# Two layers of sliding-window attention and a token-mixing MLP on one core: another order of operations and another choice of engines

## The chip, the core and the metric

The kernel runs on one core of one Trainium2 chip. The metric is the device time of one execution in microseconds (us). Four engines compute: TensorE (PE; its weight loads are shown apart as PEld), VectorE (DVE), ScalarE (ACT) and GpSimd (POOL). SyncE (SP) only issues DMAs, one after the other.

## The reference

The input x has 2048 tokens of 512 numbers. The block below is applied twice, with the same weights; all data are bfloat16.

```
def _A_ref(x, wqkv, wo):
    H = 32; Dh = D // H; W = 256
    q, k, v = (x @ wqkv) split in three, 32 heads of 16
    scores = q k^T * 0.25, masked to 0 <= i - j < 256
    return softmax(scores) v, heads joined, @ wo
def _B_ref(x, w1, b1, w2, b2):
    h = _layernorm(x)
    u = gelu(einsum("bsd,sf->bdf", h, w1) + b1)      # mixes tokens: 2048 -> 1792
    return (einsum("bdf,fs->bds", u, w2) + b2) transposed
x = x + _A_ref(_layernorm(x), ...)
x = x + _B_ref(_layernorm(x), ...)     # and both lines once more
```

## The kernel before

The program first builds a graph of 2477 operations and then writes them down in an order that a table gives. An operation is one compute instruction, or a few: a group of two or four matmuls, a DMA or a set of DMAs. The table `ORDER` is a packed list of 2477 pairs. `begin_order` (L42 on) unpacks it. The first number of a pair says which operation comes next, the second which of its ways is taken where it has several (`alts`). `Graph.replay` goes through the list, appends each operation to the queue of its engine, and hands out buffers: a tile gets, at its first operation, the buffer that has been free longest, and it gives it back after its last one. So the table fixes five queues, the engine of every operation with a choice, and which earlier operation a buffer is waited for. `Graph.emit` then places the semaphore waits. Each engine works through its queue in order: an operation that waits holds up everything behind it in that queue.

The work per layer is this.

- **Layer norm.** For each tile of 128 tokens, DVE takes statistics (L478, L480), POOL the power -0.5 (L491), DVE normalises (L498).
- **Queries, keys, values.** Four groups of 512 tokens. The normalised tile is turned by a DMA (L549; the first four tiles by PE), PE projects (L520), DVE or ACT takes the results out of PSUM (L585, L587, L610, L612, L651, L653). Keys go to `kbd`, where the two heads of a 32-row strip stand side by side with zeros between: through `stg` by eight DMAs (`f_kz`, L620), or by two masked instructions on DVE or POOL (L626). Values go through `vst` to `vb` by four DMAs (`f_vz`, L656).
- **Attention.** 76 score steps in each layer. PE writes scores into four PSUM banks (L710), ACT takes the exponential of them in two instructions (L725), POOL multiplies by a 0/1 mask or DVE takes a bitwise and (L746), PE multiplies with the values (L767). The quotient follows (L787 to L798), with the product on POOL or DVE (L793). The score steps keep their order among themselves.
- **Fillers.** Between two score steps PE runs projections of the next group, the output projection (L809 takes it out) and, for the first 4 and then the next 8 of 16 row blocks, partial sums of the first MLP product (`u_part`, L873, L877). In the second layer these partial sums cover 8 row blocks; the second MLP product of the first layer, too, runs as filler there (L929).
- **MLP.** `u_last` (L888) does the remaining row blocks, DVE adds the partial sum (L899), ACT does the gelu (L903), `y_block` the second product, DVE adds it to x (L929), a DMA writes the result.

The weights of the first MLP product are loaded by `load_w1` (L823) into four buffers of `w1b`, 128 KB a DMA. In the first layer's second `u_part` there are seven column groups of four loads; they are called g0 to g6 here, and g0.1 is the first load of g0. The second product's weights are loaded by L835 into `pt` and `w2b`. All loads stand in SP's one queue, along with the copies of keys and values and the turning of tiles.

Of the kernel before, what the change touches and what calls it, by code (L numbers as in the profile page):

```python
# [11 lines left out]
P = 128  # L12


ORDER = (
    'c-qxgO^EB(6+W`>WbTwZpa*)OfF3AC3kB4ofC38W6}70KfLioG1r=OSK?@fga6knIToA=A4!A)9FC0+81s5D}zyU8@@WKl(Cg8;sW-$vFrr^RXX7LuY7|JYq'
    'Jho>%Z(jah+C`6Mbg%CJ`ObH~>qaOwd7$sPNdoX|UDto1$8SXu@w@>1XTIxF#~p+GMz8;l2`0-jN@Vv<rB++^er(HNn&qRT`B4;AgE*K@r_A?l|Cz0M#@l_<'
    'R0L5Jwa!Q+R1k!Vv<d{W7A_KvTb0OvRx8!hYOUK4SlQOwhRz>GaS;4KW$Z9?sVrNDq3Et83A(JyB7Lk~P<nkPDsp1Z6h#sRfazpHDe!!+&F4IM{`|R!I|<3v'
    'mGAo}IS&9|94%+#_;j(D3KA9mKA9LM93LN3oYs@(5Qej<6ig-^Ny_uQmmTAjWurA8D+;9Zd5Z4Izs0t4c`z7CAjWaOC(Ae$y3iq{*&uc;<?1Ou<+9L1OMFwH'
    'l#%L;pAt4EaYRUoSi!%;AhfI?2*RKB`+W-!SeQ(D?~Y<SHcKtXX_%!b3{B&y7nGusX-3hzs>ug@7`h=?wx$7vV}>us8BZo-7}=6-_if<~H`jTQ=XrQSs3c4E'  # L20
    'I*^1Xq9jJql`Myh2|O8|oSqO$RrULdX_<>f`;>yBzR_v{@B+?lG$2m_E&;NvhS9ymhV*o~I6aO^C3*~n_VT>dnw>3|U(9B+PN`iznaxg4-MV{ndNel-!yaMy'
    'N0T@{9#7)g%$A1YUxm*<oA##@!-$RHM}x>HHJgUf&ay0RWi8J$-1f>o{Lo-5&}wBCt7;sVW6QGe2!gPz3qk-VC)H}D8mtUq2}>9Y82SSYxeGw8r?z9GUzC=F'
    '(^EzIImqbEcszc@gC<F=oB!~2k+nMln<5#qdcD%D5!(ivizCy%!8stLV(2=tEJD1uU7g5^q7b6#ntpM8O^6CGIPI(Iyf+&4fQQ%d0LW{uQA@IV3l8?uYL!(O'
    'jUkM}5~03NJlFFa-^QbP?|1~qD~e@tAPC0L=y!XBlKI?tj(p2UW@mxMn0|htGr{!~0BLq4eabK}?Lj;HOSjw2GWb)gm9ZvskzcOs!uuB=yq{1yx65VA^E}J-'
    'sQa#)Q(4z#nM$~ZRFa-ZZA6P93dkC5$^;l4U(5;aegX|a!es1@oiO(pq0Of2K#b;-S;cWkDI8iNnDusQw2~wYY*CU;O%oK_0H!d@m4xZkkwjI;Hbs<#tk>&h'
    'Ld!uSHJgowopvQ!19g=T8RcEoA(+oVYy?j9MG$VR+3eDMgb)lm9q6|6yseMNgUaCZ80g9vPi>!C7Ntp|Fm`Z&l3-hi;*%0pHB}%bUH1cD_dH5@9LP*_#yXby'
    'w1pI6tcJ)`-b#6N>oAIbT5=qRRjY??89faI2W-~@o-tWg<R=IlL!!vCETs|y70wl9xzsdeWk*LxGYx=~&gYga4F-eu0At#{ILpx+7}V>7!A#3CLYS|r;U9kA'
    '#sv;wf$M@&E(1&^wZE<Wm#-^V6_s6FT!^aj7_P1iW6ps__{G_9xI9x;b#dmp1Gf*9{Ah}_gHPdbI2v*YoQ>Olf-HspC*#R@wQoyWD&}xR$aUcgl3Ie+ZZ@0q'
    '1UuPyk|Z_MBqp*j`z2%SnU_GbS#6Av^R=3o)WmYxab4y*wh%aSHwXg&)PGyo8HXrSpoX<diRE&!P)-SfCzuhVCzx}LM^5U-d9&4=KWZ%VT+<Ex@p9ShJo;k>'
    'GNoS}(bp+oMq#0&6$M<>qMR3nk1@4vL7<?4s+yzcKRE_s5PFGuFg<eJJ!kkP01|01h<F3jmC`1j8CtDWQPievWtrG)@_Z`wP@SNgUo|c-FO^QNC}(HcsGT8I'  # L30
    '6BIEps@0_0m8(@<$5e$l3_~n^&-dg~sU#ZMrfK6bDkiMXBX`?8W#~M`oRfKp=U3!JEDTB4B~8;-4UYv8Rb{yZeRz60;(5~RF-6Xmj!ZJC|B)mUR9qsI6TDF%'
    '5JkLKW}JX>e29TF44&YfbA5e%$WN8Mi;K?)A>A(e(Cz*i^%Odt4hM}^tAbWfE4^M7$(p9A8JHxot3)?-FbvZ$Kz*t@rj2{+E9Yb)2xWM@%BLubc+b1?&<7ud'
    'oHG0DU;nf(ul}*<ot(h&f+&<o5=v98HW6`hp2NpN3-vee=D8{eAIiT&_6P!e(5?c5@^A10s#f2RDtPzBWye8b_J8F&j_2Iu+{zq;3@_iw1jmCcbrB{05#Q?f'
    '(Yc(<a5u6?9EazyyBjLX!c%q94uFcXZl+gedv-oU%w-HTfd&#D>Z2qX)>c<hT1h%d+sdj*t&%1US&qxqa;(TK3`b)!9t;SuZm;VH7+REzDDK&IVEa}SnW^a}'
    'cv<kikN1*hxGENgi85hm8fF4BbWNmfK~(zyDe0h8^ht&0X{y(QIMyS%LQ96mAEBB@Vsu4mNJ#%&UCQ8{k4B@;ktFf0>tj*Sdo`XyehzfJ7?0ca1i9k$w62zG'
    'ie`*QooW?zQFGl!qn@@F<2W7;hjFtRcN0W4Q7x<F`!_!cf=ZyOb^J--*{-Uq2nnhsphmCKO<rjsd?(}Xf1$0*oxat_y1MtmWU^Z)yUXk@PdMZ>_EV0mm)!>_'
    '?&D71TW^Ss`!_W#_gB@e?Qa&|+w4V(H?8Y2#o~74y7|5p)<v=KGM`_==gX~7xVHql!0p1s-9ziP<aY79`F=2ke03CF<G61XIF7ql;W%ywcJ859g^g2%!cH66'
    '?R@b>xJu#X`7*j}UHys!ZXx=nZWX>+Klchu=e})LtclO<hIe-%j^p6}*bZNPDtkb!&Hws!%d`hMwYQycGZbK3KE$89i^AsnCJdWMti)y|DcmZlc2jTNaWC77'
    '#oJ1;c++}NJixD;KYSe=6mQ2B*WoSRb;G*4UF4=*9~qBce37*~dGu1hHqaC{+O~#jzp!`b^Fs!{kb2xcswsKxR&lqwyGCS3<hXk<tPalYc(egz0}Jd*=#J~R'
    'WB1@*<BKj8H&OkXWL^_wt3rj%Y;H$LA8f*Xoe17tQiT;e3NIVMaW75QS4m%PSJ1WscXw@aJ9>OOU~_}q@pP*z#d{a-_K>?G^WT*i?p0<yJOcNs`*Ppm<hyt6'  # L40
    'Rt&f;;4fHV`zoxf+jrr1@@6h~N1~VBo&OVo{}2Aq9P0'
)  # L42

def begin_order(n):
# [965 lines left out]
```

## Time and profile before

| what | value |
|---|---|
| three runs | 436.65, 437.78, 437.89 us (median 437.78) |
| the profiled execution, its own time | 437.46 us |
| its span, first to last instruction | 435.7 us |
| granted TensorE clock | 1.000 |
| PE busy | 422.4 us, 6185 matmuls |
| ACT busy | 315.7 us |
| DVE busy | 319.3 us |
| POOL busy | 188.3 us |
| 128x512 matmul, shown duration | 381 ns |
| exponential of 128x1024, shown duration | 1047 ns |
| bytes moved by DMA | 46.17 MB |

The shown duration of a matmul overlaps the next one. Six 128x512 matmuls in a row take 1.40 us in the chain, and 26 of them 5.72 us, so they start 0.216 us apart. The same holds for exponentials: 40 in a row take 36.97 us in the chain, 0.92 us each. A stretch is read by the engine that has no idle time in it.

### The profile page before, as it was taken

Reading aid. Unit: us, or ns where it says so; the run is one execution under the profiler, and the core shown is the slowest. Engines: PE = TensorE matmul, PEld = TensorE weight load, DVE = VectorE, ACT = ScalarE, POOL = GpSimd, SP = SyncE. Lnnn points to the kernel's source line nnn. Section 1 sums busy time; section 2 is a strip of 40 time slices with the busy share of each in tenths; the row PEclk is TensorE's granted clock in tenths of the full one; section 3 lists DMA queues with packets and bytes.
Section 4 is the critical chain, followed back from the end, with each engine's and each line's share of the span. In section 5 each row is a group of like instructions: output and inputs, shape, how many; then the busy total and the mean of one; then the engine's idle time right before and its main releaser. Section 6 shows DMA issues by size and latency. Waiting matters only on the chain.

```text
span 435.7 us, 14338 instructions
## 1 busy us (share of the span) xinstructions
PE 422.4 (97%) x6185; PEld 188.9 (43%) x6185; DVE 319.3 (73%) x620; ACT 315.7 (72%) x360; POOL 188.3 (43%) x280
## 2 busy tenths in 40 slices
PE   8989889999989999999999999999999999999997
PEld 6544333443334444444344444444444444445443
DVE  7999888798786888656778998779879757522133
ACT  6999999999996952604989999999999970520000
POOL 5967757656662510010374566777455241000000
PEclk9999999999999999999999999999999999999999
DMA  8763223212054248742462550331224144776433
GB/s 253 196 126 72 58 66 85 62 25 56 15 139 114 72 124 228 204 101 48 89 146 67 129 128 5 63 75 23 47 61 116 53 136 124 194 201 181 138 89 129
DMA packets 103002, 46.17 MB, mean 106 GB/s; under 512 B 33308, under 2 KB 102940, under 8 KB 102940
## 3 DMA queue, kind: packets, MB, share of 16 engines
q1 hardware_dynamic: 102940, 45.26, 40.7%
q8 instruction: 49, 0.80, 0.8%
q14 instruction: 13, 0.11, 0.1%
HBM read 33.56 MB, written 2.10 MB: 82 GB/s over the span
## 4 chain that ended last, share of the span: by engine, by line
PE 77%; ACT 19%; DMA 2%; DVE 1%; issue 0%; SPq 0%; POOL 0%
PE PS L520 54%; ACT pt L725 18%; PE PS L888 8%; PE PS L710 8%; PE PS L767 7%; DMA w1b<-in_B_w_dram 1%; DMA x_sb<-in_A_x_dram 0%; SPq L823 0%; DVE stats L478 0%; ACT kbd L595 0%; DVE stg L610 0%; POOL rstd L491 0%; DVE oT L798 0%; ACT xhT L569 0%; ACT qT L587 0%
## 5 line engine op out<-in xcount | busy, mean ns | idle before, releaser
L725 ACT ACTIVATE pt<-PS 128x1024 bf16<-128x1024 f32 (+1 forms) x304 | 280.6, 1035 | 12.8 <-PE PS L710 11.9
L746 POOL TENSOR_TENSOR pt<-pt,ldm 128x256 int32<-128x256 int32 (+2 forms) x199 | 132.2, 684 | 92.8 <-ACT pt L725 92.1
L520 PE MATMUL PS<-xh_sb,w1b 128*128 128x512 bf16 x280 | 70.0, 381 | 1.6 <-DMA w1b<-in_B_w_dram 1.5
L520 PE MATMUL PS<-xhT,wqkv 128*128 128x512 bf16 (+1 forms) x288 | 67.8, 357 | 2.0 <-ACT pt L725 1.3
L520 PE MATMUL PS<-uT,w2b 128*128 128x512 bf16 (+2 forms) x308 | 67.5, 360 | 0.0
L710 PE MATMUL PS<-qT,kbd 32*128 32x64 bf16 (+4 forms) x1552 | 60.2, 247 | 3.0 <-ACT pt L725 1.2
L929 DVE SCALAR_TENSOR_TENSOR x_sb<-PS,bcol,x_sb 128x512 bf16<-128x512 f32 x31 | 22.7, 744 | 44.7 <-PE PS L520 44.6
L491 POOL TENSOR_TENSOR rstd<-agg,mhalf 128x2 f32<-128x2 f32 (+1 forms) x33 | 24.2, 736 | 67.0 <-DVE agg L480 66.8
L710 PEld LDWEIGHTS PS<-qT,kbd 32*128 32x128 bf16 x1552 | 22.6, 92 | 62.1 <-ACT pt L725 42.0
L787 DVE STREAM_TRANSPOSE rl<-PS 128x1024 f32<-128x1024 f32 x32 | 39.8, 1244 | 11.7 <-PE PS L767 11.6
L767 PE MATMUL PS<-pt,vb 64*17 64x128 bf16 (+4 forms) x3104 | 44.2, 248 | 1.7 <-issue 0.7
L478 DVE BATCH_NORM_STATS2 stats<-x_sb 128x6 f32<-128x512 bf16 x64 | 43.2, 682 | 0.8 <-DMA x_sb<-in_A_x_dram 0.2
L903 ACT ACTIVATE uT<-rl,bcol 128x512 bf16<-128x512 f32 x28 | 18.1, 711 | 34.7 <-DVE rl L899 34.7
L520 PEld LDWEIGHTS PS<-uT,w2b 128*128 128x128 bf16 x308 | 27.5, 98 | 31.2 <-issue 2.9
L520 PE MATMUL PS<-uT,pt 128*128 128x512 bf16 x168 | 39.7, 379 | 0.0
L767 PEld LDWEIGHTS PS<-pt,vb 64*17 64x17 bf16 x3104 | 31.8, 84 | 17.5 <-issue 8.5
L520 PEld LDWEIGHTS PS<-xh_sb,w1b 128*128 128x128 bf16 x280 | 23.6, 97 | 32.8 <-issue 6.6
L888 PE MATMUL PS<-xh_sb,w1b 128*128 128x512 bf16 x168 | 37.4, 379 | 0.0
L520 PEld LDWEIGHTS PS<-xhT,wqkv 128*128 128x128 bf16 x288 | 23.9, 97 | 29.4 <-issue 6.2
L520 PE MATMUL PS<-wqkv,xhT 128*128 128x512 bf16 x128 | 34.2, 381 | 0.0
L520 PE MATMUL PS<-wo_sb,oT 128*128 128x512 bf16 x128 | 33.1, 381 | 0.8 <-ACT pt L725 0.5
L746 DVE TENSOR_TENSOR pt<-pt,ldn 128x256 int32<-128x256 int32 (+2 forms) x67 | 27.3, 420 | 5.2 <-ACT pt L725 5.1
(64 smaller groups left out, 332.6 us busy)
## 6 DMA issues: line engine op xcount, KB each, us to landing
w1b<-in_B_w_dram SPq DMA_DIRECT2D x112, 128.0 KB, 3.0
w2b<-in_B_w_dram SPq DMA_DIRECT2D x70, 128.0 KB, 3.0
pt<-in_B_w_dram SPq DMA_DIRECT2D x42, 128.0 KB, 3.0
vb<-vst SPq DMA_DIRECT2D x64, 68.0 KB, 2.1
out_dram<-x_sb SPq DMA_DIRECT2D x15, 128.0 KB, 1.8
x_sb<-in_A_x_dram SPq DMA_DIRECT2D x3, 512.0 KB, 5.9
kbd<-stg SPq DMA_DIRECT2D x88, 16.0 KB, 1.9
wqkv<-in_A_wqkv_dram SPq DMA_DIRECT2D x4, 256.0 KB, 4.1
```

Of the source, the lines that this page charges most:

```text
L478: op("vector:stat", lambda e: e.bn_stats(st[:, 0:6], x_sb[:, t, :]), reads=[f"x{t}"], writes=[("st", i)], cost=dve_cost(512))
L491: op("gpsimd:rstd", lambda e: e.tensor_tensor(rstd[:, t0:t1, 0], agg[:, t0:t1, 1], mhalf[:, 0:1].to_broadcast([P, t1 - t0]), op=ALU.pow), ...
L520: return e.matmul(o, lhsT=w, rhs=x, start=start, stop=stop, skip_group_check=True)
L710: last = e.matmul(bank(tt[r // 2], r % 2)[:, base + c0 * 64:base + (c0 + n) * 64], lhsT=kbd[32 * r:32 * r + 32, tk.slot, o, jj].rearrange( ...
L725: op("scalar:exp", lambda e, ts=ts, tp=tp, i=i, cols=cols: e.activation(probs(tp)[:, i, 0:cols, :], pair(ts)[:, :, 0:cols].rearrange("p r ...
L746: return e.tensor_tensor(v, v, m, op=by)
L767: last = e.matmul(bank(t, h)[32 * r:32 * r + 17, i + q0 * 64:i + (q0 + n) * 64], lhsT=vb[64 * h:64 * h + 64, tk.slot, jj, 4 * o + r, :], r ...
L787: op("vector:od", lambda e, t=tod, tr=tr: e.transpose(rl[:, tr.slot:tr.slot + 2].rearrange("p a b -> p (a b)"), pair(t)), reads=[(tod, i) ...
L888: last = e.matmul(bank(tu, tt), lhsT=v()[:, sc - b0, k0 + tt * P:k0 + (tt + 1) * P], rhs=xh_sb[:, sc, :], start=(sc == b0), stop=(sc == NT ...
L903: op("scalar:gelu", lambda e, ft=ft, tt=tt: e.activation(uT[:, ft, :], rl[:, tmps[tt].slot], ACTF.Gelu_apprx_tanh, bias=b1col[:, ft:ft + 1 ...
L929: op("vector:resy", lambda e: e.scalar_tensor_tensor(x_sb[:, t, :], bank(ft), b2col[:, t:t + 1], x_sb[:, t, :], op0=ALU.add, op1=ALU.add), ...
```

## The change

Only the table `ORDER` is different; every other line stays, line numbers too. The graph is the same 2477 operations with the same dependences.

```
 ORDER = (
-    'c-qxgO^EB(6+W`>WbTwZpa*)OfF3AC3kB4ofC38W6}70KfLioG1r=OSK?@fga6knIToA=A4!A)9FC0+81s5D}zyU8@@WKl(Cg8;sW-$vFrr^RXX7LuY7|JYq'
...
+    'c-pmAPl)5@6@Rk7>3*Aj1Dc|M7PLhH6?9NQ0TmQbKmi35(1HUF_@ICbK8WIi4_;6~0Uca$zzYs2;DQ%iP{9Qi9B{w|7v|uDTlV0C3qH(Y0zSAffuYP{4twac'
...
 )
```

Unpacked, the two tables compare as follows (number of operations on each engine, where it has a choice):

| operation | before | after |
|---|---|---|
| attention mask (L746) | POOL 199, DVE 67 | POOL 178, DVE 88 |
| keys into `kbd` (L620, L626) | SP 11, DVE 9, POOL 4 | SP 8, DVE 7, POOL 9 |
| quotient's product (L793) | POOL 21, DVE 11 | POOL 22, DVE 10 |
| queries, keys, values and partial sums out of PSUM (L585 to L590, L610 to L614, L651 to L653, L873, L875) | DVE 107, ACT 16 | DVE 109, ACT 14 |
| keys straight to `kbd` (L595, L600) | DVE 7, ACT 2 | DVE 6, ACT 3 |
| zeroing a half of `kbd` at the start (L468, L469) | ACT 2, POOL 1 | ACT 1, POOL 2 |
| the ones column of `vst`, a part of the mask (L442, L463) | DVE 1, POOL 1 | POOL 1, DVE 1 |

In all, 120 operations change their engine. ACT has 358 operations before and 356 after, DVE 611 and 630, POOL 269 and 255, SP 311 and 308.

PE's queue holds the same 928 operations. The 152 score steps keep their order. From score step 12 to 60, and from 84 on, the operations between two score steps are the same but for single fillers that move by a step. Before step 12 products with the values and projections stand elsewhere by one or two steps. In the two MLPs the groups of two matmuls are interleaved in another way: products of the second kind begin earlier beside the last ones of the first kind.

SP's queue is the one that changes most. Around the second `u_part` of the first layer:

```
before: g1.1 (18.8 us) ... g1.4 (61.8) ... g1.2 (88.2) ... g2.1 (102.7), keys x2,
        values, g6.2, g0.3, g2.3, g2.4, g0.2, g1.3, g0.1, values, g0.4, g2.2, ...
after:  g1.2 ... g1.1 ... g1.3 ... keys x2, g1.4, ..., g2.2, ..., keys, g2.4, one w2 load,
        g0.1, values, g0.2, g5.1, g0.3, g2.1, g0.4, g2.3, ...
```

The exponentials of a score step's two halves change places in many steps. One eviction of values that stood on ACT at 118.05 us (L653) stands on DVE behind L791 and ahead of L610. On DVE at the start, one L478 and one L480 stand ahead of the L585 that was at 9.60 us, and the L585 of 11.84 us goes to ACT in place of the one that was there at 11.81 us. In the last MLP the matmuls of the fifth loaded column group of `u_last` stand ahead of those of the seventh in PE's queue; they stood behind them before.

More of the change, by code (lines that the diff above doesn't have):

```diff
@@ L15 @@
 ORDER = (
[L16 to L39, printed above, removed]
@@ L40 @@
-    'WB1@*<BKj8H&OkXWL^_wt3rj%Y;H$LA8f*Xoe17tQiT;e3NIVMaW75QS4m%PSJ1WscXw@aJ9>OOU~_}q@pP*z#d{a-_K>?G^WT*i?p0<yJOcNs`*Ppm<hyt6'
-    'Rt&f;;4fHV`zoxf+jrr1@@6h~N1~VBo&OVo{}2Aq9P0'
+    'c-pmAPl)5@6@Rk7>3*Aj1Dc|M7PLhH6?9NQ0TmQbKmi35(1HUF_@ICbK8WIi4_;6~0Uca$zzYs2;DQ%iP{9Qi9B{w|7v|uDTlV0C3qH(Y0zSAffuYP{4twac'
+    'Ju|j<v-#6(pDpXt_rCAbd++yq@3~Rpn>=_Bh6Hq!;>W}*m%;Oj#iII=>$-HL*v_xuU9;Eic0n_Kt$UB+n5|YT+D)9qsX5iSP*!|WIvs!Lk47WwJxg=lOp#^F'
+    'vOp4XTUU}K!me>32;H7At5)0oC+(!&>1G{K^20c`T<JkjsZi>dsm7EdacPAR+j?kOqIM)pk{}UDmSv(4o*a`I&u(NgKFtUvWH9IrSk}L~zLE$CYw^#ot_p=h'
@@ new lines @@
+    ';H)lYCZ)&cXXJD|8;{4+>6D=SJsY2neP1pOhO(TH^BPIJr1Mnx?DNH9p(tbqGYKFF&g0<AAPfE)^s|1@PZc7|oem+C(zYbETDs~$+ipa$`1>dfL#`<_DJ7rK'
+    'u!gT;r`1AGt=6gxU#Nd<+jeRAXf)!A1*`u78aJ8PuGcM>%f2(UdQIE*Bi{!T3Z}6^!1WBnu?^RA?e`1|-8BpYK-JWdWepfmNYfs4b(QCtA_LR`L{SXG6R52)'
+    '<V+GvrAtxd#@^^YJ(}Ay%2fK6ESo5c_8ewPt0hS?x+w?{$6bgZyH3-qtLx|Ob{JlTjm8<ApPik>|LR^ql3bAK>iqotAJeIyB=h-V(eS+K91ok%=hf=PeBlJn'
+    ';;Z?f-_OZuCT7#=Unp8^_<okO`~6nS?{un$5gYANDQdU8Cx1W^B+W*XF+Gae?=(#aT({vg8nS%ZYzjV;fAgQ2Uz^QJrFsxR5elUOAUTJHVyWMU4>2NQ45nq8'
@@ new lines @@
+    'x<M)Xt*EHp^clSnM8c0x_$<?985k2-yVXV!0BZO~MjQv6z;<gjM8p=E;2habMYliTi<BBJXtJW1rgBZGZCs8gb7E47l5w1#sVR?0DynkSNaJR+*Gh=oI64YN'
+    'p<W9}z?X^dAC)LYYzt1IU|Uw@8M2cc;TFppT12`prTsoh)ATtI;Q6tsf6eRKwYCs1FUV|7OyGwZOeTz_y&(*Tqi(U^|MS{wxhr%#aqIwCjhbNDb{I|p9wS9Y'
+    'j$H7(M~}dDL9~q~2zc}<FY!F`!7UYBQ9_Vmfu^ihYwp6R+X+LQ0)n~UY(~v`os>$k5)_MpUn*J*G=M0!EQJzkXcbK_mkV0S15I@`W>Z7e^hB>wN$RSKpS9cR'
+    'fQVg5k;)pa*W*}-qFSw3w7~RC-gS$Gx@(#Q(^zBI*9-~mdXv&A^2R+AylFOLLkx+mMq}}BqKrmMV*ROP+s$S<ibS5pCeI53Vj`SW0>lakk)-F!L(CBXx^(G@'
@@ new lines @@
+    'ZNsx?E_vp@YuiaeZO69bnBMma-rGSCyfd#jPQ`JH2ym@N-5{W}OkC}qw>3>ObX_GpFY}7RBU@OLQJ|tAP>K~t0hrA&nI1@3Ivz+vl*xFAi6($3{ZSN!w4QdV'
+    's!AG-K>~%i*HbRO!9%e=hydeoB!5*G#R3#+t}L-*38cm42^=q%7Yvrm`;s)u1|v){NlG!6<GF3Gk?QHc7!9-jXjCrqFb3**Ubp*8j=*OFsVOI|R_jTx*F&;M'
+    '*VjGLgHM;sFpOZaNSa9JAUvH+#@XcbaTG>zLty1H<^az`G4@!gUiUovedajt^M#UcIVh4@*hCUk)lyZ!jMlFKOcz!wSPHVB0=&sEA_z=&<@K-9)DY7&5#Z}-'
+    'FV?kVZFQmnU35A!A(&*07x-kHB;boukxK=#dM-RII8IrVuqVtt?;}e2iJ=`0D4oq`h&&RZRHFBhpUCcqSjjWSo`TnRJI+%lP0S*+-)tud;vwU)^5;@YX+K4K'
@@ new lines @@
+    '(>~f;M_Fj`tc8sPpc2+=wOYN~>()V+wT)jsfZ_m_NRzqi8mc=kRS_b+fnhWZeVwBkasU_tE>Izw8@6G{hCz=t4ZUUrkruJLEtg9{H}rmgfH|!H^Q6l<h&{nq'
+    'L<p@ImCGkQ6vc8`5>G@r90~%*(iD2?T)n33^73?iU*d*%OqSsu^!!gxCzBAkC+qrzW`7ECqu;Nl2#Oc4>$HWL;`%=J*OZt<a~+-6?DvRiMwrKj`L;eFX!ir`'
+    'A%c%#=iGG(aKv+mEx%d9Ih<Xck;Q8DZ-Si_yRi7>aC|yBH4IT7>taXCGK4g1eenf6`65X^NAT8do`&_u^`?UXdR&33rfarc0k`lmCbVU#hUVC&<2tH(t=i6}'
+    'h>*7)Je2r{4|tyE7&~Uz3YAWRSyF}P!DVRMjDcZI0sAU;EdmTLstFfNSxTWG42F@=?3KIo^<hwNgpDMwHlx_DRNAdpy;k+2a)6prtzN8##ZnQ<BJX;9(`|aO'
@@ new lines @@
+    '8v#bk25R~~Q^C+ccb$S)t-8{=qA2rnsi2s^OD<-mwN5UIg`Flt8R;yny3uO&yw;?vt7NtES&gnDI}(cxzQN8*OIHwz=Ryhl^7XmRW}&9@(_&8@PU>tdr2{FO'
+    '&(pLvDi)iC27xTgW|^U+aCVA+emdCfu+_?j+=`;8L5piRk#1qNBimK*B~vP3H`6o|s#Pfnq>Aq8m^||4&&@hYYg_T!JpEMRIN&ySxc%i|H{`gRHMc@uIsi$2'
+    'Fo_R@+YZpWp8*yp+)r+2@W`zi?r|Ggk5IP5djR?TT6y%wcFp$8{Jq`yyCg^Oh3oH&lFz+*4@y2yArHB44-asA&qv!mHzC<Yhuh4qU0nxs6V%&n9K0UMAH851'
+    'cZb<_d<RnwzSWn_eD1*Wz1zOAH^$$d^U`4)960_8Qtj-6-1h<Z^5fBWaP~(M{73KQxV<dk?oPOi_|9{V`zi2pua6zCM~)9}JL+w|`)h7FliTFaj$OG!?%fh>'
@@ L42 @@
+    'v*ajukapXP+f4p^S9ZAlwA#V94)hxw-12JOS~u6GvTRY<jJAaa<pp52Wd(0HzU1>Scz8d*IeepjL3y_`e;0<0L%YN|48n_~zSZ4n?j0&~d%oV=5q9mw&%T9U'
+    'WLtF)A93R4mHCZ2pT8OG*RfkC^SCX)hwjV1-v*52UQXDx8M)1lgDP^E%iGV6GTWuOJrcY!A6}JShqJl6KE)lr`KB7bM5dpRue-v>-3|8Y!cAq^y=YH!Qx&&%'
+    '-deWRk;A2THTeHm9e!9SevlE|{~pQj)9oX=7t+1Ba|eKI%*}0o@Rr+hAeZBA@!Boq_QAVVeqYai4S4()i034d'
 )
```

## The prediction

> **What bounds the kernel now.** The first view is busy time by windows that follow the stages.
>
> ```profile
> 9.00:117.00 108.00, 101.38 (x2036) 44.36 (x2036) 94.26 (x189) 107.49 (x122) 76.00 (x111) 1.00 0.37 82
> 117.00:160.00 43.00, 41.27 (x875) 18.90 (x873) 34.29 (x63) 35.88 (x39) 19.04 (x26) 1.00 0.37 98
> 160.00:215.00 55.00, 55.00 (x315) 23.80 (x300) 37.06 (x67) 22.15 (x30) 6.03 (x9) 1.00 0.56 146
> 215.00:356.00 141.00, 140.67 (x2520) 59.34 (x2519) 116.06 (x229) 135.13 (x149) 81.79 (x117) 1.00 0.32 79
> 356.00:436.00 80.00, 76.85 (x384) 36.19 (x382) 31.11 (x52) 9.84 (x16) 1.39 (x2) 1.00 0.52 148
> ```
>
> The columns after the window are its length, then busy time of PE, PEld, DVE, ACT and POOL, then PE's granted clock. From 9 to 117 us ACT is idle for 0.51 us of 108, PE for 6.62: the exponentials set the pace. From 117 on it is PE: 1.73 idle to 160, none to 215, 0.33 to 356; the 3.15 in the last window are mostly its ends. The clock is 1.00 everywhere. The change leaves PE's 928 operations and all exponentials in place, so an order can only win idle time: 0.5 us of ACT before 117, 1.7 + 0.3 us of PE to 356, and little behind.
>
> The second view, the chain of waits, agrees, and names one load:
>
> ```profile
> 42.99 36.97 ACT pt L725 x40
> ...
> 125.75 4.67 DMA w1b<-in_B_w_dram
> 130.46 1.90 PE PS L520 x8
> ...
> 160.17 5.72 PE PS L520 x26
> ```
>
> The third, the timelines of PE, ACT and SP around that place, gives its price and its cause:
>
> ```profile
> 130.46 1.90 PE L520 MATMUL PS<-xh_sb,w1b 128*128 128x512 bf16 x8 [1.52 <-DMA w1b<-in_B_w_dram]
> ...
> 132.74 1.94 ACT L725 ACTIVATE pt<-PS 128x1024 bf16<-128x1024 f32 x2 [2.26 <-PE PS L710]
> ...
> 116.00 1.24 SPq L620 DMA_DIRECT2D kbd<-stg  x2
> 118.67 3.81 SPq L656 DMA_DIRECT2D vb<-vst  x4
> 122.52 3.71 SPq L823 DMA_DIRECT2D w1b<-in_B_w_dram  x7
> ```
>
> PE stands 1.52 us, and ACT 2.26 behind it. The load is g0.1, issued at 125.75 as the last of the seven: SP first spent its time on a copy of keys and 3.81 us on a copy of values. It then took 4.67 us to land, one of the slowest of its line:
>
> ```profile
> DMA to landing us min/median/max: 2.1/3.0/4.9
> ```
>
> **The change, part by part.** The sum starts from the profiled execution's own 437.46 us, 0.32 under the median of 437.78; the runs lie 1.2 apart. About 0.3% (1.3 us) is what a measurement of this kernel can tell from no change, so faster means under 436.47 and slower over 439.09.
>
> *g0.1 goes ahead of the values copy.* In the new SP queue it stands behind the copy of keys (done at about 117), one w1 load and one w2 load, about 0.5 us each. It is issued at about 118, and even with 4.9 us it lands by 123; its matmuls would begin 0.216 us (the spacing of matmuls) after the ones at 128.34 and 128.55, so at 128.8. The hole goes: 1.52, and the 0.381 shown for the last matmul before it shrinks to its 0.216, another 0.17. PE has 0.33 us of idle time from 160 to 356, so what is won here is carried to the end. **-1.7.** The three loads fill the 1.43 us for which SP stood before the values copy (117.24 to 118.67). The copy itself waits for an eviction that now ends on DVE at 118.99 instead of 118.64, so it begins 0.33 later: the last of its DMAs, issued at 120.66 before, then lands by 120.66 + 0.33 + 3.2 (the longest here) = 124.2, and its reader, a PV product, starts at 124.79. Behind it the loads g0.2, g5.1 and g0.3 are needed later than g0.1 was, each at least 3.5 us from issue to use. If one of them is late, the hole moves instead of going; that is the first rival.
>
> *The start.* One L478 (0.69) and one L480 (0.18) are put ahead of the L585 of 9.60, with 0.65 to 0.8 us delay. That is the queries of the second score step, whose matmuls start at 10.11; they can then start at 10.9 or 11.0, and the exponentials that wait for them stand ready from 11.95, as the four at 9.03 end then. With 0.8 us from scores to exponential that leaves 0 to 0.3 of ACT idle, and as much again where the exchange of L585 and L587 near 11.8 (0.38 and 0.40) reaches the exponentials. ACT sets the pace here, so it passes one to one. Bounds 0 and +0.5; **+0.3**, nearer the upper one since queues don't step aside.
>
> *An eviction of values moves from ACT (118.05, 0.59 long) to DVE.* DVE is idle for 0.70 from 118.29 to 118.99 between L791 and L610, so it fits. ACT's time is worth something only if ACT sets the pace, and from 117 PE does: **0**, bound -0.65.
>
> *120 operations change engine.* DVE gets 6.2 us more, POOL loses 5.7, ACT 1.1, from their rows' means. In 9 to 117 DVE goes from 94.3 to about 99.6 of 108. What covers it: DVE still has 8 us over, and between the end of a mask and the PV product that reads it lie 3.5 us at the median; under 0.6 in 11 of 99. PE waits for POOL's masks before L767 four times, 2.2 us in all, at places where PE waits for ACT anyway. **0**; without the cover see the third rival.
>
> *Keys.* Three copies fewer go through SP, at 5.5 to 6 us of its time each, and POOL does five more. This eases SP where weight loads queue. The copy through SP that is left with the least room lands in about 7.3 us against 7.8 to its reader: **0**.
>
> *A fetch of instructions.* PE stops for 0.54 us in the middle of one product at 116.31, with no operation to wait for. The same 2,107 matmuls stand ahead of it afterwards, so it may stay: **0**, bound -0.54.
>
> *The last MLP.* The fifth column group of `u_last` now goes ahead of the seventh, so its buffers' loads have less time. Before, from the issue of a load to its reader there were 3.7 us or more. Laid out with 0.216 us a matmul, six loads now have 2.8 to 3.5, mean 3.2: two of the fifth group (sixteen matmuls, 3.3 to 3.5, less 0.5 for the second, which SP issues later) and four further on. What landings took there, first `w1b` from 369 to 378, then `w2b` and `pt` from 377 to 406:
>
> ```profile
> DMA to landing us min/median/max: 2.1/2.8/3.8
> ...
> DMA to landing us min/median/max: 2.2/2.9/3.4
> ```
>
> At the medians only the tightest is missed, by 0.1. Bounds 0 and 6 x (3.8 - 3.2) = +3.6; **+0.2**, by the medians.
>
> These loads move 128 KB. The Trainium skill, "DMA: Bandwidth & Descriptors", section "Anatomy of one DMA — SWDGE (gpsimd) path", gives about 2.0 us plus the bytes over 436,000 a microsecond, for another issuing path; an estimate by it is 2.3 us, by which no load is late and this term is 0. The trace's medians are 0.5 us above it, so the trace does not agree.
>
> Sum: 437.46 - 1.7 + 0.3 + 0.2 = 436.26, so **436.3**.
>
> **The rivals.**
>
> *No difference.* The load's hole closes and something else takes its place: one of the loads behind, or ACT, which has only 7.1 us idle in 117 to 160, 2.26 and 1.09 of them at this hole. Or the hole is not in every run: 4.67 us of landing is far above the median, and with 3.0 the load would have been there at 128.8, in time. Then only the start's cost is left: 437.46 to 437.8, and with half of the gain 436.9. For it: the hole's load is a slow draw. Against: the draw's median just meets the need, and the spread of the three runs is of the hole's size. Taken over, 436.5 to 439.
>
> *Slower, by the last MLP.* PE is the only engine at work there, so each late load is paid in full. With the burst's 3.8 for all six it is 437.46 - 1.7 + 0.3 + 3.6 = 439.7. It decides (over 439.09) from a mean landing of 3.2 + 3.03 / 6 = 3.7 us. Against it: 2.8 and 2.9 as medians. For it: the DMA engines are busiest here, and the tight loads stand in bursts.
>
> *Slower, by DVE and POOL in each other's way.*
>
> ```profile
> L746 POOL TENSOR_TENSOR pt<-pt,ldm 128x256 int32<-128x256 int32 x141 | 102.9, 743 | 61.1 <-ACT pt L725 60.6
> ...
> L746 DVE TENSOR_TENSOR pt<-pt,ldn 128x256 int32<-128x256 int32 x49 | 20.8, 431 | 5.2 <-ACT pt L725 5.1
> ```
>
> Of POOL's masks of 128x256, those alone have a median of 0.727 us; nine that overlap a DVE mask have 0.904. In 9 to 117 there are 18 more masks on DVE. If each costs its neighbour 0.18 and PE's product and then ACT waits for it, that is 3.2: 436.3 + 3.2 = 439.5. It decides from 0.155 each (2.8 / 18). If a mask held POOL for DVE's whole 0.431, it would be 7.8, and 444. Against it: POOL has 32 us idle there, and its waits are for ACT.
>
> The Trainium skill, "SBUF — State Buffer", section "SBUF: two separate sides", says that a DVE instruction with two SBUF inputs and a GpSimd one that reads SBUF lock each other out for the whole instruction; that rule speaks against this change. The nine rows agree in sign, and at 0.18 they show less than a full lock.
>
> **How the numbers follow.** The forecast, 434 to 436.47, gets 0.43: one measured hole with a cause that the new queue removes, at a gain near the bound. No difference gets 0.26. The late loads get 0.20, DVE and POOL 0.11. The lower end is 433.8: 437.46 less 1.7, 0.65, 0.54 and most of ACT's 0.5 before 117, less 0.3 for the draw of a run. The upper end is 440.5, the two slower cases with 0.8 for a spread between runs. Likeliest alone: 435 to 437. Faster 0.43, same 0.26, slower 0.31.
>
> **What would show it.** Right: no wait of PE L520 for `w1b` near 130, g0.1 issued near 118, ACT without the 2.26, and the chain from 160 on shifted earlier by 1.3 to 1.7 with PE at 55.0 of 55 behind. The start: ACT idle 0.2 to 0.4 between 9 and 22. The last MLP: PE's waits for DMA in the last 80 us in sum, 0.2 by the forecast and 3.6 by its rival. The masks: POOL's mean over 743 and ACT below 107 of 108 by the third. Wrong: the first score step of layer two no earlier than before, or PE idle by over 1 us anywhere behind 160.

## The result, and the profile after

The changed kernel is slower: 438.48 us, median of 20 executions, against 437.20 of 20 executions of the kernel before; ratio 1.003, 95% interval 1.0016 to 1.0045. The forecast was 436.3. The profiled execution of after took 437.81 us (span 436.1), so it is one of the quicker ones. The 20 executions of before lie 2.7 us apart, those of after 4.6, and so one profile of each can't show a difference of 1.3. In the runs below, a few executions far outside the rest (480 to 2283 us; one of 528.44 had a granted clock of 0.755) are left out of the ratios.

The first reading is the windows of after, columns as in the prediction.

```profile
9.00:117.00 108.00, 97.89 (x2029) 44.88 (x2049) 98.22 (x199) 107.13 (x123) 74.06 (x109) 1.00 0.35 80
117.00:160.00 43.00, 41.67 (x873) 19.40 (x880) 33.21 (x63) 36.11 (x39) 20.75 (x29) 1.00 0.41 110
160.00:215.00 55.00, 53.43 (x296) 23.19 (x300) 35.69 (x67) 24.32 (x33) 7.55 (x12) 1.00 0.50 136
```

DVE went from 94.3 to 98.2 (about 99.6 was forecast), and ACT from 107.5 to 107.1 of 108, as forecast. The third row is new: before, PE was busy for 55.00 of 55. (This trace has 6117 of 6185 matmuls, so busy PE is a little low elsewhere too; waits are safer to read.)

The second reading is the timeline around the old hole, PE, then ACT, then SP.

```profile
128.36 2.44 PE L520 MATMUL PS<-xh_sb,w1b 128*128 128x512 bf16 x10
...
131.18 1.94 ACT L725 ACTIVATE pt<-PS 128x1024 bf16<-128x1024 f32 x2 [0.67 <-PE PS L710]
...
118.92 1.70 SPq L823 DMA_DIRECT2D w1b<-in_B_w_dram  x1
120.67 2.62 SPq L656 DMA_DIRECT2D vb<-vst  x4
```

PE runs through, and ACT idles 0.67 instead of 2.26: g0.1 is issued at 118.92, ahead of the values. At 148.4 us PE is 1.50 ahead of the profile of before. The third reading, PE's timeline further on, shows where this went.

```profile
187.08 1.04 PE L520 MATMUL PS<-uT,pt 128*128 128x512 bf16 x4 [1.09 <-DMA pt<-in_B_w_dram]
...
377.35 1.90 PE L888 MATMUL PS<-xh_sb,w1b 128*128 128x512 bf16 x7 [0.52 <-DMA w1b<-in_B_w_dram]
```

The first is in the first layer's MLP, of which the prediction said nothing, the second in the last MLP. Before, PE ran through at both places; at the second its timeline has one unbroken row:

```profile
373.91 10.52 PE L888 MATMUL PS<-xh_sb,w1b 128*128 128x512 bf16 x48
```

In SP's and DVE's timelines the cause of the first can be read:

```profile
171.82 0.47 SPq L835 DMA_DIRECT2D pt<-in_B_w_dram  x1
179.49 1.40 SPq L835 DMA_DIRECT2D w2b<-in_B_w_dram  x3
180.93 0.47 SPq L823 DMA_DIRECT2D w1b<-in_B_w_dram  x1
181.44 0.47 SPq L835 DMA_DIRECT2D w2b<-in_B_w_dram  x1
181.96 1.50 SPq L835 DMA_DIRECT2D pt<-in_B_w_dram  x3
...
178.79 0.68 DVE L899 TENSOR_TENSOR rl<-PS,w2b 128x512 f32<-128x512 f32 x1
```

SP issues nothing from 172.3 to 179.49. The `w2b` load at the head of its queue needs a buffer that holds a partial sum, and DVE's L899 reads that one at 178.79, until 179.47. The load of `pt` that PE wants sits six places behind the head: issued at 182.48, landed 4.56 us later. Nobody needs the load at the head before 185.40. The old queue stands there for 2.4 us only:

```profile
169.58 2.48 SPq L835 DMA_DIRECT2D pt<-in_B_w_dram  x5
174.50 0.37 SPq L835 DMA_DIRECT2D w2b<-in_B_w_dram  x1
```

### The profile page after: what moved, and what is told of

Same layout as the page of the kernel before. It is cut to its first block, busy times and chain, and to the rows that moved or that the text cites. A ratio compares the mean times of both kernels' runs of the same rounds, so it can differ in the third digit from the quotient of the medians.

```text
span 436.1 us, 14244 instructions
## 1 busy us (share of the span) xinstructions
PE 412.8 (95%) x6117; PEld 188.4 (43%) x6185; DVE 324.3 (74%) x637; ACT 315.4 (72%) x359; POOL 183.2 (42%) x271
## 4 chain that ended last, share of the span: by engine, by line
PE 70%; ACT 19%; DMA 4%; DVE 3%; issue 2%; SPq 2%
PE PS L520 48%; ACT pt L725 19%; PE PS L710 8%; PE PS L888 7%; PE PS L767 7%; DMA x_sb<-in_A_x_dram 1%; DMA pt<-in_B_w_dram 1%; DMA w1b<-in_B_w_dram 1%; DVE stats L478 1%; DVE rl L899 1%; SPq L835 1%; DMA vb<-vst 0%; SPq L656 0%; DVE xh_sb L498 0%; ACT L959 0%
## 5 line engine op out<-in xcount | busy, mean ns | idle before, releaser
L746 POOL TENSOR_TENSOR pt<-pt,ldm 128x256 int32<-128x256 int32 (+2 forms) x178 | 119.5, 689 | 96.3 <-ACT pt L725 96.0
L520 PE MATMUL PS<-xhT,wqkv 128*128 128x512 bf16 (+1 forms) x276 | 66.1, 356 | 4.4 <-ACT pt L725 2.3
L520 PE MATMUL PS<-xh_sb,w1b 128*128 128x512 bf16 x266 | 66.9, 380 | 2.2 <-issue 1.7
L491 POOL TENSOR_TENSOR rstd<-agg,mhalf 128x2 f32<-128x2 f32 (+1 forms) x33 | 23.0, 698 | 61.1 <-DVE agg L480 61.0
L478 DVE BATCH_NORM_STATS2 stats<-x_sb 128x6 f32<-128x512 bf16 x64 | 43.0, 685 | 1.2 <-DMA x_sb<-in_A_x_dram 0.4
L520 PE MATMUL PS<-uT,pt 128*128 128x512 bf16 x165 | 41.0, 379 | 1.5 <-DMA pt<-in_B_w_dram 1.1
L746 DVE TENSOR_TENSOR pt<-pt,ldn 128x256 int32<-128x256 int32 (+2 forms) x88 | 35.3, 421 | 6.5 <-ACT pt L725 6.4
L888 PE MATMUL PS<-xh_sb,w1b 128*128 128x512 bf16 x164 | 37.4, 379 | 0.8 <-DMA w1b<-in_B_w_dram 0.5
L520 PE MATMUL PS<-wqkv,xhT 128*128 128x512 bf16 x116 | 32.2, 380 | 2.1 <-issue 1.1
L793 POOL TENSOR_TENSOR ul<-rl,rc 128x512 bf16<-128x512 f32 x22 | 23.8, 1081 | 22.7 <-DVE rc L791 21.8
```

The source lines that it names most:

```text
L478: op("vector:stat", lambda e: e.bn_stats(st[:, 0:6], x_sb[:, t, :]), reads=[f"x{t}"], writes=[("st", i)], cost=dve_cost(512))
L491: op("gpsimd:rstd", lambda e: e.tensor_tensor(rstd[:, t0:t1, 0], agg[:, t0:t1, 1], mhalf[:, 0:1].to_broadcast([P, t1 - t0]), op=ALU.pow), ...
L520: return e.matmul(o, lhsT=w, rhs=x, start=start, stop=stop, skip_group_check=True)
L746: return e.tensor_tensor(v, v, m, op=by)
L793: f_n = lambda e, tr=tr, tl=tl: e.tensor_tensor(ul[:, tl.slot].rearrange("p (q x d) -> p x q d", x=2, d=16), T(tr)[:, :, :, 0:16], R(tl).u ...
L888: last = e.matmul(bank(tu, tt), lhsT=v()[:, sc - b0, k0 + tt * P:k0 + (tt + 1) * P], rhs=xh_sb[:, sc, :], start=(sc == b0), stop=(sc == NT ...
```

## The experiments

All compare with the kernel before on the same chip. The theory after the first profile: what was won by 150 us was lost in the two MLPs, at one load each. The rivals were that loads set the pace there whatever their order, that the loss is spread over the many engine choices, and that chance made the profiles. A cut between the orders is made where both have the same work on PE behind them.

**One stretch at a time.** First, the new first part alone:

```diff
-up to 151.6 us: order of before
+up to 151.6 us: order of after
 from there on: order of before
```

> The new order up to the product that starts at 151.6 us before (150.4 after), the old order from there on, the whole first MLP and layer 2 included. Theory A (the gain is made in the first 150 us and lost by the new queues of the two MLPs): up to the cut the two profiles differ by -1.5 us, and with the old first MLP this is kept to the end: 437.2 - 1.5 = 435.7. Theory B (the first MLP's loads set the pace whatever their order, so PE that comes earlier only waits longer for them): nothing is left, 437.2. Theory C (the loss lies in the many engine choices of the first 150 us and the profile of after was a lucky draw): 438 or more.

Measured: 437.03 against 436.98 us, ratio 1.0001 (0.9985 to 1.0016). Its profiled execution was 1.1 us ahead of the profile of before at 148 us and stayed so to the end. So in this execution nothing is lost in the old MLPs (theory B has no support there), yet the median shows no gain, and the 435.7 of theory A lies outside the interval (436.3 and up): the 1.5 was measured from one execution of before.

```diff
 up to 151.6 us: order of before
-151.6 to 216.7 us: order of before
+151.6 to 216.7 us: order of after
 from there on: order of before
```

> The old order up to 151.6 us, the new one for the first MLP and the start of layer 2 (to 216.7 us), then the old one again. Theory A: SP stands 7.2 us for one load of the second product's weights, whose buffer holds a partial sum until L899 reads it; the loads behind it come late and PE waits 1.1 us plus the 0.2 that overlapping matmuls hide: 437.2 + 1.3 = 438.5. Theory B (PE came too early): PE comes 1.5 us later here, so the loads are in time, 437.2. The profile also shows whether the hole of 1.5 us at 130 us and the stop of 0.54 at 116 us, both in the untouched part, are there in another execution.

Measured: 439.99, ratio 1.0051 (1.0031 to 1.0070). The loss is there, but the cut adds to it: at 156.33 us PE waits 0.95 for an L877 that stands behind two L498 on DVE, which no whole kernel shows. Of the wait at 187 us it has 0.43. And in the untouched part the hole at 130 us is 1.03 us, not 1.52, and the stop at 116 us isn't there. In layer 2, again in the old order, PE waits 0.85 at 290.59 for a copy of values that took 3.8 us to land; the profile of before has no wait there, the tenth run 0.25.

```diff
 up to 355.8 us: order of before
-from there on: order of before
+from there on: order of after
```

> The old order up to 355.8 us, the new one from there on: the last MLP alone. The profile of after lost 0.7 us here, 0.52 of it at one wait for a load of the column group that was moved ahead. Theory A: 437.2 + 0.7 = 437.9, a PE wait for w1b near 377 us again. Theory D (the 0.8 us by which the medians differ more than the two profiles lies here, because six loads are tight and landings scatter): 438.7. Theory B says nothing here: 437.2 if that wait was chance.

Measured: 436.84, ratio 0.9997 (0.9983 to 1.0010). Theory A's 437.9 lies outside the interval. Its profile has the wait, 0.89 us at 376.67, and the hole of before at 0.49:

```profile
129.16 1.90 PE L520 MATMUL PS<-xh_sb,w1b 128*128 128x512 bf16 x8 [0.49 <-DMA w1b<-in_B_w_dram]
```

Profile and median disagree; more on this below.

**The load behind SP's stop.** In the whole new kernel, one load of SP's queue is moved:

```diff
 ... pt, pt, w1b, pt,
+pt (read at 187.08),
 w2b (waits for L899 until 179.47), w2b, w2b, w1b, w2b, pt,
-pt (read at 187.08),
 pt, w1b, w2b, ...
```

> The new order with one load moved: the one that PE waited for at 187.08 us (its reader is the first of two products with pt there) stands in SP's queue ahead of the load that waits 7.2 us for its buffer, instead of six places behind the head of that stop. Theory A: it is issued near 172.3 instead of 182.5, PE's wait of 1.1 us goes: 438.5 - 1.3 = 437.2. Theory B (the loads set the pace): another load is as late, 438.5.

Measured: 438.38, ratio 1.0027 (1.0006 to 1.0047). In the profile the mend works: issued at 172.75, landed 10.5 us ahead of its reader, no wait, and PE as far ahead at 218 us as at 148. The profiled execution took 437.02. The median does not follow: theory A's 437.2 lies just outside the interval (437.24 and up). So there should be further places with a loss, which the first profile of after did not show.

**One load in the old order.**

```diff
 SP, near 102.7 us:
-w1b (read at 136.52)
+w1b g0.1 (read at 130.46)
 SP, near 125.8 us:
-w1b g0.1
+w1b (read at 136.52)
```

> The old order with two loads of w1b exchanged in SP's queue: the one PE waits for at 130.46 us (issued at 125.75) goes to the place of one that was issued at 102.67 and is first read at 136.52, and that one takes its place. Nothing else changes. In three executions of the old first part the hole was 1.52, 1.03 and 0.49 us. Theory A (the hole is worth its mean of 1.0 and the 0.2 that overlap hides): 437.0 - 1.2 = 435.8. Theory B (what is won ahead of the MLPs is lost in them): 437.0.

Measured: 436.98 against 437.11, ratio 0.9993 (0.9981 to 1.0005). The wait for the load is gone from the profile. The interval goes to -0.8 us; a gain of 1.2 lies outside it.

**All but one stretch.** The new order with the old first MLP:

```diff
 up to 151.6 us: order of after
-151.6 to 216.7 us: order of after
+151.6 to 216.7 us: order of before
 from there on: order of after
```

> The new order, with the old one for the stretch from 151.6 to 216.7 us (the first MLP and the start of layer 2). Theory A (SP's stop of 7.2 us there is what costs, 1.3 by the profile): 438.4 - 1.3 = 437.1. Theory B (loss spread over other places): 438.4.

Measured: 437.80 against 437.11, ratio 1.0017 (1.0003 to 1.0030): some 0.6 less than the whole change, half of theory A, with intervals of 0.6 on either side.

```diff
 up to 355.8 us: order of after
-from there on: order of after
+from there on: order of before
```

> The new order up to 355.8 us, the old one from there. In three profiles the new last MLP cost 0.7 to 1.05 us against the profile of before, with a PE wait of 0.52 to 0.89 for the same load of the column group that was moved ahead; timed alone it cost nothing (-0.14). Theory A (the wait is there in most executions): 438.4 - 0.9 = 437.5. Theory E (the old order loses as much there in its usual execution, and the profile of before was a good one): 438.4.

Measured: 439.51, ratio 1.0064. This tells nothing of the last MLP: at the cut a load that the new order issues early is late, and PE waits 2.03 us for it at 358.06.

```diff
-up to 30.8 us: order of after
+up to 30.8 us: order of before
 from there on: order of after
```

> The old order up to 30.8 us, the new one from there. In three profiles the new start costs 0.13 to 0.3 us at 30.8 and 0.32 to 0.5 later on against the profile of before; two other executions of the old start were 0.18 and 0.07 behind it. Theory A: 438.4 - 0.3 = 438.1. Theory F (the start also decides how later fetches and loads fall, and is what costs the 0.8 that no profile shows): 437.3 or less.

Measured: 439.49, ratio 1.0056. Here too the cut costs: by 93 us its profile is 1.96 behind, 1.5 more than the new kernel's, and it isn't read for the start. Behind that it serves as one more execution of the new order.

**The last MLP again.** The third kernel a second time, and with an exchange in SP's queue:

> The same program as the third run (old order up to 355.8 us, new last MLP) once more, for a second sample. In five profiles of the new last MLP it cost 0.65 to 1.07 us, in four of the old one 0.0 to 0.05, yet the third run's median showed -0.14 (interval about -0.7 to +0.4). Theory A (the cost is real, that median was a good draw of the part ahead): 437.1 + 0.9 = 438.0, a PE wait for w1b near 377 again. Theory E (no cost on average): 437.1.

Measured: 437.54 against 437.39, ratio 0.9996 (0.9977 to 1.0014), a wait of 0.60 at 376.97.

```diff
 SP, 372 to 373 us:
-w1b (read at 378.66), w1b, w1b (read at 377.35)
+w1b (read at 377.35), w1b, w1b (read at 378.66)
```

> As the run before it, with two loads of w1b exchanged in SP's queue, so that the one PE waits for is issued 1.0 us earlier and the other, read 1.3 us later, in its place. Theory A: the wait of 0.5 to 0.9 and its 0.2 go from the profile, 0.7 less than the run without the exchange. Theory G (the loads of this burst are limited by the DMA engines, each landing 4 us after issue): the wait moves to the next load, and the time is the same.

Measured: 437.14, ratio 0.9998 (0.9976 to 1.0020). The wait went to the next load of the same group, 0.40 at 376.74, as theory G has it; whether the DMA engines are what holds these loads up was not tried.

**Both mends, and two exchanges in the old order.** The new kernel with the edits of the fourth and the tenth run:

> The new order with the two loads mended: the one of the first MLP ahead of SP's stop (as in the fourth run) and the exchange in the last MLP. Theory A: 438.4 less the mean wait in the first MLP (1.09, 0.43, 0.47, 0.45 in four profiles, mean 0.6, and 0.2 each for overlap) and 0.7 in the last: 436.9, the time of before or a little less. Theory H (the new order loses elsewhere by scatter, as the fourth run's 438.38 beside a profile of 437.02 suggests): 438.

Measured: 437.62 against 437.39, ratio 1.0008 (0.9988 to 1.0028), between the two theories. No wait near 187; near 377 it moved to the neighbour load, at 0.99.

The fifth run's kernel with one more exchange:

```diff
 SP, 372 to 374 us:
-w1b (read at 379.09), w1b, w1b, w1b (read at 377.80)
+w1b (read at 377.80), w1b, w1b, w1b (read at 379.09)
```

> The old order with the exchange of the fifth run (the load of the hole at 130 us) and one more in the last MLP, where the load that lands 0.05 to 0.17 us ahead of its reader in three profiles changes places with one that is read 1.3 us later. Theory A (each takes away a place where scatter of landings reaches PE): 436.4 to 436.8, half a microsecond under before. Theory B: 437.1.

Measured: 437.24, ratio 0.9997 (0.9977 to 1.0018). Behind 100 us PE waits no more than 0.21 us at a time in its profile up to 434 us, and it is no faster that can be shown.

**The two kernels again, and a cleaner cut.**

> The kernel before, unchanged. Ratio 1.000; its distance from it is what a comparison of this kind makes out of nothing. Profile: if the hole at 130 us is of its usual size, 0.5 to 1.0 us (five executions of the same part had 1.52, 1.03, 0.49, 0.88, 0.60), its execution's time is 436.7 to 437.2.

Measured: 437.50 against 437.08 for the same program, ratio 1.0019 (1.0002 to 1.0036). So 0.2% can come out of nothing, and single ratios above have to be read with that. The hole was 0.50 us this time; PE's timeline has beside it a stop that names no wait.

```profile
116.95 0.30 PE L767 MATMUL PS<-pt,vb 64*17 64x320 bf16 x1 [0.62 <-issue]
...
130.09 1.90 PE L520 MATMUL PS<-xh_sb,w1b 128*128 128x512 bf16 x8 [0.50 <-DMA w1b<-in_B_w_dram]
```

> The kernel after, unchanged: 1.3 us more than before. Profile: PE waits 0.45 to 1.1 us near 187 for the load behind SP's stop, 0.5 to 1.0 near 377, no hole at 130.

Measured: 438.70, ratio 1.0034 (1.0020 to 1.0049). PE waits 0.29 us at 187.37, less than was expected, and 0.72 at 378.46. This execution of after (438.94 us) shows a place that the first had only by a margin. PE and SP:

```profile
255.88 0.40 PE L710 MATMUL PS<-qT,kbd 32*128 32x256 bf16 x8 [0.47 <-DMA kbd<-stg]
...
248.23 6.20 SPq L620 DMA_DIRECT2D kbd<-stg  x8
```

It is a copy of keys in layer 2. Before, DVE made it in two instructions, done 7 us ahead of its reader. The new order gives it to SP, where eight issues take 6.2 us; it lands at 255.75, and what is queued behind it, a turning of tiles, comes 5 us later than before:

```profile
251.80 4.51 SPq L549 DMA_TRANSPOSE xhT<-xh_sb  x3
```

Here it begins at 257.16.

```diff
 up to 328.7 us: order of after
-from there on: order of after
+from there on: order of before
```

> The new order up to 328.7 us, the old one from there. Theory A (the last MLP and its first loads cost 0.9 on average): 0.4 over before, that is the first MLP's 0.8 less 0.4 for the first part. Theory E (the end costs nothing on average): 1.3 over before.

Measured: 438.29, ratio 1.0031 (1.0013 to 1.0049): the whole loss is there without the new end.

```diff
 up to 328.7 us: order of before
-from there on: order of before
+from there on: order of after
```

> The old order up to 328.7 us, the new one from there. Theory A: 0.9 over before. Theory E: 0.

Measured: 437.52, ratio 1.0010 (0.9997 to 1.0023). Its profile is not read.

**The loss up to 328 us mended.** The kernel with the cut at 328.7, and two edits:

```diff
 SP: the load read at 187.08 stands ahead of the stop, as in the fourth run
-SP:  kbd<-stg, eight DMAs (L620), layer 2, near 248 us
+DVE: kbd<-stg, two instructions (L626)
```

> The new order up to 328.7 us and the old one from there, with two mends: the load of 187 us ahead of SP's stop, and the copy of keys of layer 2 on DVE (two instructions there, no DMAs). Theory A: PE waits for neither, 0.7 + 0.2 us less than the kernel without the mends, and at 328.7 us 0.3 ahead of the mean of the old order: 436.8. Theory H (the loss up to 328 us is scatter that these waits don't make up): no less than the other run, 438.

> The new order up to 328.7 us, the old one from there, once more: 438.0, with PE waits near 187 us or 255 us in the profile.

Measured on one chip: 436.98 with the mends (ratio 1.0001, 0.9988 to 1.0014), 438.27 without (1.0025, 1.0009 to 1.0040). The two edits together are worth the whole loss, 1.3 us. The profile without them shows three waits on PE that the profile with them does not have (its execution took 439.55, 1.3 over the median of its kernel):

```profile
187.46 1.04 PE L520 MATMUL PS<-uT,pt 128*128 128x512 bf16 x4 [0.75 <-DMA pt<-in_B_w_dram]
...
255.77 0.40 PE L710 MATMUL PS<-qT,kbd 32*128 32x256 bf16 x8 [0.24 <-DMA kbd<-stg]
...
265.56 0.61 PE L520 MATMUL PS<-xhT,wqkv 128*128 128x512 bf16 x2 [1.56 <-DMA xhT<-xh_sb]
```

The third is a turned tile for the next projection, issued at 261.12 behind the copy of keys. PE waits for it in this execution alone; in eight others with the copy on SP it landed 0.2 to 1.1 us ahead of its reader, with the old queue some 5 us ahead. A fourth wait of this execution, 0.60 at 159.33 for a load of `w1b`, is one that neither edit touches. SP's timeline without and with the mend:

```profile
248.08 6.24 SPq L620 DMA_DIRECT2D kbd<-stg  x8
...
257.05 5.34 SPq L549 DMA_TRANSPOSE xhT<-xh_sb  x3
```

```profile
247.39 0.47 SPq L823 DMA_DIRECT2D w1b<-in_B_w_dram  x1
...
250.39 8.67 SPq L549 DMA_TRANSPOSE xhT<-xh_sb  x3
```

The turning begins 6.7 us earlier, and the tile lands 2.2 us ahead of its reader.

**The stretches over all profiles.** PE's time between points with the same work behind them, against the first profile of before, in us (mean, and smallest to largest). Executions whose cut adds a wait in a stretch are left out of it.

| stretch | forecast | old order | new order | new less old |
|---|---|---|---|---|
| to 93 us | +0.3 | 0.32 (0.00 to 0.72), 8 executions | 0.49 (0.25 to 0.92), 10 | +0.2 |
| 93 to 127 | 0 | -0.32 (-0.78 to 0.10), 8 | -0.36 (-0.80 to 0.13), 11 | 0.0 |
| the hole, 127 to 131 | -1.7 | -0.69 (-1.03 to 0.00), 6 | -1.21 (-1.58 to -0.75), 11 | -0.5 |
| first MLP, 148 to 218 | 0 | 0.00 (-0.02 to 0.03), 9 | 0.90 (0.48 to 1.80), 6; mended 0.00 to 0.10, 3 | +0.9 |
| layer 2, 218 to 328 | 0 | 0.16 (-0.06 to 1.20), 9 | 0.37 (-0.17 to 1.80), 9 | +0.2 |
| from 328 | +0.2 | 0.02 (-0.02 to 0.09), 9 | 0.89 (0.71 to 1.13), 7 | +0.9 |

The last column adds up to 0.8 up to 328 us, where the medians gave 1.3, and has 0.9 behind it, where the medians gave nothing. So the places are read from the profiles, and what they are worth from the medians. The 0.9 of the first MLP is 0.7 without the execution that had the extra wait at 159 us, and the 0.2 of layer 2 hangs on one execution of each order (1.20 and 1.80).

## Why the prediction was wrong, point by point

**The hole: right in place and mechanism, wrong in size.** The step that failed is "**-1.7**", the price of one execution taken as the price of all. The hole's wait in six executions of the old queue was 1.52, 1.03, 0.49, 0.88, 0.60 and 0.50 us, mean 0.84. And the new order doesn't run through there always: in nine of eleven executions PE stops inside the same group of matmuls, where no wait stands, for 0.15 to 0.78 us, the mean over all eleven being 0.34. What is left is 0.5. The traces tie these stops to a transfer on the queue that they call "instruction" (last section); it lies there in the old order too, hidden under the wait for the load, and with that load exchanged the fifth and the twelfth run still stop for 0.25 and 0.19. So this is the first rival, "something else takes its place", in part, and its second reason ("4.67 us of landing is far above the median") as well. The new first part alone gave 1.0001. The sum also started from 437.46, the execution that was profiled; the median of 20 is 437.20.

**The start: right as far as can be told.** By the profiles the order costs 0.2, forecast 0.3, within the scatter of either order; ACT's idle time from 9 to 22 us went from 0.03 to 0.38, as said. A little more went into it than was worked out: the L478 that now stands ahead of L585 waits 0.24 for a load of x.

**The first MLP: missing.** PE's idle time from 160 to 215 us was read as "none", and with that the step ended; the loads of that stretch were not laid out against their readers, as those of the last MLP were. In seven executions with the new queue PE waited there each time, 0.28 to 1.09 us, with another 0.2 from the lost overlap; in three with the load ahead of the stop, never; in nine with the old order, never. The prediction's own sign of being wrong, PE idle by over 1 us behind 160, stood in the first profile of after.

**Keys: the step "0" failed.** The prediction counted copies ("Three copies fewer go through SP") and so missed that three in layer 2 went the other way, from DVE to SP, one of them at a place where SP had no 6 us to spare. "7.3 us against 7.8 to its reader" was worked out for another copy; this one lands 7.0 to 7.6 us after its first issue, and its reader starts after 7.2 to 7.7, waits included. PE waited for it in five of nine executions, 0.24 to 0.51 us. Together with the load of the first MLP it is the loss up to 328 us: with both mended the median is that of before, without them 1.3 more, beside each other on one chip. How the 1.3 divides between the two is open. By the profiles most of it is the first MLP's; but the fourth, sixth and eleventh run, which have this copy on SP (and the new end) but no late load in the first MLP, came out at 1.0027, 1.0017 and 1.0008, so by times the copy and what it delays may well cost as much.

**The last MLP: late loads, as the second rival had it, but not the one that was worked out, and the size is open.** "**+0.2**, by the medians" is too small by the profiles: 0.9 in seven of seven. The tightest load in the working, the second of the fifth group ("less 0.5 for the second"), was in time: it stands near the start of a burst of ten issues, and where its landing is recorded there it took 2.3 to 2.8 us. PE waited for the second load of the seventh group, by the order table the seventh issue of the burst, which had 3.5 us to its reader and took 3.94 in after. So the step that failed is one median for all loads of a burst. By the Trainium skill's figure for one DMA ("DMA: Bandwidth & Descriptors", "Anatomy of one DMA — SWDGE (gpsimd) path"), estimated at 2.3 us for another issuing path, no load would have been late; the traces do not agree. But by the times the new end costs nothing that can be seen: 0.9997, 0.9996 and 1.0010, timed behind the old order. The old order may have waits at its end that nine profiles happened not to show, or the profiled executions differ there; the runs don't settle it.

**DVE and POOL: the third rival fell.** POOL's masks of 128x256, rows by form of before and after:

```profile
L746 POOL TENSOR_TENSOR pt<-pt,ldm 128x256 int32<-128x256 int32 x141 | 102.9, 743 | 61.1 <-ACT pt L725 60.6
```

```profile
L746 POOL TENSOR_TENSOR pt<-pt,ldm 128x256 int32<-128x256 int32 x127 | 93.6, 746 | 65.9 <-ACT pt L725 65.6
```

The mean rose by 3 ns; 3.2 us over 127 masks would have been 25. The condition did not come about: from 9 to 117 us DVE has 24 masks after against 18 before, six more and not "18 more", and of POOL's masks of this shape four overlap one of them, before and after. Those four have a median of 0.84 and 0.86 us, the others 0.73, so a mask on DVE beside one on POOL does cost about 0.1 us, equally often in both orders. The lock of the Trainium skill ("SBUF — State Buffer", "SBUF: two separate sides") shows here as no more than this 0.1 us.

**The other zeros held.** The stop of 0.54 at 116 us is there in some executions only: it was 0.39 to 0.64 at the same product in six of nineteen executions, three of them with the old order there and three with the new. The eviction moved to DVE cost nothing by itself. The copy of the values began not 0.33 later but 2.0 (120.67 against 118.67), so they land close to their reader, with waits of 0.18 and 0.19 in two executions.

**The range** took in the result; the side was wrong. What the forecast won is by the profiles under a third of its price, and no median shows it; the two losses that outweighed it stood in stretches that were called full.

## What to carry to other kernels

A wait of PE for a DMA changes from execution to execution: price its removal by the landing's median, or by several executions, not by the one that was profiled, and ask what stops PE at the same place once it is gone. In a stretch where PE has no idle time, nothing can be won, but a new order can lose there: lay every load out from issue to reader, and look at what stands at the head of its queue, for one load that waits for its buffer holds back every one behind it. When work is moved to a queue, count what it delays there: eight short DMAs cost the tiles queued behind them 5 us, though the copy itself was hardly late.

## What the runs showed of the hardware

PE stops at fixed places inside a group of matmuls, with no operation to wait for, in some executions of a program and not in others: near 116 us for 0.39 to 0.64 us, near 129 us for 0.42 to 0.78 in five of eleven with the new queue. The traces have packets of 16 KB on a queue that they name "instruction", one every 4 to 10 us in that part. In all eleven of these stops PE goes on 1.35 to 1.55 us after the end of such a packet. Near 116 us PE reached the place 0.50 to 0.74 us after the packet's end in the six executions that stop, and 0.9 or more after it in the thirteen others, which stop there for 0.20 at most. So the stop fits the name that the prediction gave it, a fetch of instructions that comes too late; no run changed the fetches to test it. A load of 128 KB lands 2.1 to 2.3 us after its issue when it is the first after an idle time of SP, and later in a row of issues half a microsecond apart: after SP's stop in the profile of after the fifth took 5.0 us and the seventh 4.6. Two sets of executions of the same program on one chip differed by a ratio of 1.0019.
